# A linear-attention and maxout-FFN kernel: gate weights fetched in two parts each, a halved last tile, and a new order of the steps

## The chip, the core and the metric

The kernel runs on one core of a Trainium2 chip. The metric is the device time of one execution in microseconds (us), lowest first. A core has five instruction streams: TensorE (PE, matmuls), VectorE (DVE), ScalarE (ACT), GpSimd (POOL) and SyncE (SP, which here only issues DMAs). POOL also issues DMAs, those that change the type on the way. All DMAs of the core share 16 DMA engines.

## The reference

Two stages. The first is a recurrent attention with decay over 4 batches, 8 heads, 768 steps and 48 dimensions per head; the second a maxout feed-forward layer on the 3072 tokens of 384 features that the first gives.

```python
for t in range(S):                                  # S = 768
    state = alpha[:, :, t, :, None] * state + k[:, :, t] (outer) v[:, :, t]
    y[:, :, t] = q[:, :, t] @ state
x = y with heads side by side                       # 3072 x 384
h = max(max(x @ w1, x @ w2), x @ w3)                # w: 384 x 768
out = h @ w_out                                     # w_out: 768 x 384
```

Everything comes in and goes out as float32.

## The kernel before

**Tiles.** The sequence is cut into chunks; one *group* `n` (12 of them, three chunk pairs for each of the 4 batches, the batches taking turns) is 256 tokens and two *units* `u = 2n, 2n+1` of four heads each. The products run in fp16.

**Maxout as differences.** The kernel keeps w1 and turns w2 and w3 in place into `w2 - w1` and `w3 - w1` (tile `wcat`). Then `h' = max(0, x(w2-w1), x(w3-w1))`, and the lost part `x w1` goes past the maximum: `out = h' w_out + x (w1 w_out)`. The product `past = w1 w_out` is made once; for it w1 has to be turned (`w1T`) on PE.

**Steps.** `Plan.step` records each piece of work with its operands; nothing is issued then. The steps that the text speaks of, by kind:

- `load` (SP): q, k, v or alpha of a group, 384 KB in rows of 384 bytes (group 0 in halves of 192 KB). `weights` (POOL): a weight, cast from fp32 to fp16 on the way.
- per group: `aa` (alpha pair product), `la` (its logarithm, ACT), `hp` and `e` (chunk totals, PE and ACT), `G` (decay factors).
- per unit: `Lp` (PE, sums of logarithms), `L0` (DVE), two `exp` (ACT), two `qk` (products, DVE or POOL), `v` (scaling, ACT or POOL), `tp` (PE, 16 transposes), `qkT` (DVE), `A` (PE, scores), `LA` (DVE, mask).
- per group: `pp` (PE, new state), `Zp`, `Z`, `add` (DVE or POOL, carry the state), `yi` and `ya` (PE, outputs from the state and within the chunk), `xb` (ACT or DVE), `xp` (PE), `xT` (ACT or DVE): the layer's input, turned.
- once: `d` (DVE, the six differences, of 256 columns each), `wt` (PE, turn w1), `w1T` (copy), `mp` (PE, w1 w_out), `past` (copy).
- per group of the layer: six gate steps `gp(n, j, g)` (PE, six matmuls of 128x128 on 256 columns; `j` is the block of 256 hidden columns, `g` the difference), `h0` and `h1` (the maxima), two `op` (PE, three matmuls with `past` and six with w_out), `ob` (copy of the output tile of 128 tokens) and `out` (SP).

**Order.** The order of all steps is written out in the table `ORDER`. A token such as `254P1` means step 254, on PE, in PSUM bank 1; the letters P, V, A, G and S stand for PE, DVE, ACT, POOL and SP. `Plan.emit` issues the steps in this order, so each engine runs its own steps in the order of the table, and waits where an operand isn't there. Step numbers count the calls of `Plan.step`; `WAFTER` only says at which point of the recording a weight's step is numbered; its place in time is the table's alone.

What a line number in the profile stands for: L262 load, L272 weights, L281 `d`, L294 `wt`, L307 `mp`, L324 `aa`, L329 and L334 `la`, L389 `Lp`, L393 `L0`, L398 `exp`, L403 `qk`, L421 `tp`, L429 `qkT`, L441 `A`, L449 `LA`, L472 `pp`, L509 `yi`, L531 `ya`, L551 `xp`, L575 `gp`, L584/L586 `h0`, L591 `h1`, L603 and L606 the two halves of `op`, L618 `out`; L243 and L247/L249 are helpers for copies and scalings.

Of the kernel before, what the change touches and what calls it, by code (L numbers as in the profile page):

```python
# [10 lines left out]
FP32 = mybir.dt.float32  # L11
# [15 lines left out]
6S 0S 3S 1S 2S 52S 5S 7S 8V 9A 4S 10A 11G 17P0 54S 18V 13A 53S 19A 14P1 98S 28P2 12A 20A 55S 29V  # L27
15A 22V 100S 30A 31A 21V 99S 56V 101S 24P3 16G 143S 58A 32V 145S 57A 33V 74P5 144S 59P6 25V 62P7
35P0 146S 23A 63V 205S 26P2 64A 36V 272S 65A 34A 206S 75V 37P0 67G 27V 207S 60A 40P47 77A 274S 76A
61G 339S 66V 208S 42V 78G 69P2 38V 273S 39G 79V 41V 73G 81P5 68A 102G 82V 70V 83P0 80G 104A 44P4  # L30
85G 84V 86P56 45P2 87V 71P0 88V 46A 119P3 72V 103A 47P5 90P2 49A 120V 91P4 122A 193P0 92V 95A 105P1
121A 89V 108P4 93P2 48A 43V 96P3 50P6 123V 51A 94A 124V 109V 126P5 111A 97A 195P7 189V 106A 187V
196A 262P2 127V 321P3 194A 188V 128P5 110A 113V 254P1 112G 129V 258P7 255A 130G 329P0 115P4 192V
330A 197P1 107G 116V 114A 125G 331P6 198A 190V 117P4 325P0 322A 118V 147G 148A 256P1 191V 149A
131P34 263A 257V 153P5 259A 264P2 154V 133V 326A 132V 164P1 260P7 156A 265V 327P0 165V 261V 167A
135P3 323P2 166A 332V 155A 136P7 324V 169G 201P1 140V 158G 150P6 199P5 202A 137A 157V 151A 168V
160P2 328V 171P6 203P1 159A 170G 172V 200A 161V 173P6 204A 175P05 209G 174V 162P2 333P1 211A 163V
276G 277A 210A 218P6 269P7 334A 152G 219V 539S 278A 176V 275S 134V 221A 340S 177V 220A 141P2 229P3
138P1 341S 285P4 222G 230V 179P0 139A 266P6 142V 406S 231A 286V 342S 232A 223V 288A 234G 279P1
180P2 270A 267V 287A 212P3 178V 392P7 181A 233V 213A 296P6 225P4 280A 215G 184A 297V 236P2 290G  # L40
394P1 226V 299A 298A 237V 301G 182P0 393A 388P4 183V 344A 185P5 343G 238P2 395V 224A 227P6 336P0
186A 228V 289G 235A 389A 214G 239V 217G 390P1 337A 216G 345A 292P5 338S 300G 240P74 473S 293V 363P0
352P2 396P3 408S 353V 241V 474S 354A 463P5 391V 397A 268S 242G 398P6 335S 291A 282G 243V 409S 461P7
464A 281G 364V 302G 407S 399V 366A 459P3 284G 271S 365A 244V 476S 245P1 355A 246P5 460V 307P60 671S
357G 247P 462V 605S 294P2 251A 465P4 283G 295V 248A 356G 252P7 411A 455P5 253A 308V 368G 457P1 456A
466V 249P2 359P6 410G 458V 250A 303P3 346P5 529P2 304V 310G 412A 525P1 360V 309G 347A 530A 367G
305P3 311V 369A 361P5 521P7 306V 526A 349G 350G 358A 312P2 523P0 351G 522A 362V 543G 313P1 413P3
419P4 430P7 314P 414A 431V 370P5 420V 433A 467P3 524V 315A 435G 371V 318A 421A 477G 372P0 422A
374P25 545A 470P6 436G 479A 375V 478A 348G 373V 376G 432A 379P4 434G 480P2 471A 403P7 468A 424V
377V 486P0 319P1 423G 404A 531P6 487V 378V 488A 405S 380P3 527P7 481A 532V 608S 320A 541S 489A 381P  # L50
609G 528V 544A 475S 426P1 437P5 382A 540S 415G 316P0 427V 503G 400P7 317A 438V 416G 385V 383P4
552P1 401V 386P2 384A 591P0 483V 387A 402S 553V 484G 428P5 672S 592A 439P3 675G 497P7 555A 655P2
440V 554A 425G 593P0 611A 485G 498V 589P1 500A 418V 429V 491G 546P3 499A 653P4 587P7 417G 654A 594V
441P56 547A 676A 490V 563P4 533P3 442V 588V 443G 444G 656V 661P0 534A 501G 564V 447P5 535S 663P7
590V 662A 606S 492G 677A 446P2 445V 657P3 674S 565A 502G 664V 542S 566A 493P0 448P 658V 472S 482G
556G 504P6 607S 494V 508P4 624A 469S 659P3 452A 449V 610A 618P0 505V 595P1 450P5 453P2 596V 597P6
451A 454A 509V 536P7 660V 511G 549G 619V 568G 598V 621A 506P1 495P4 620A 678P3 551G 537A 725P6 496V
569G 679A 538S 684P0 612P7 719P3 557G 673S 685V 507V 665P4 567G 550V 686A 629P5 695P1 548V 599P2
510V 613A 720A 681V 623V 666A 615V 683V 723P7 622G 696V 630V 698A 602P3 724V 631A 614G 558G 687A
726V 635A 688G 721P4 697A 600V 603A 512P7 700G 601S 513P0 722V 632A 625P1 667S 514P 604S 626V 699G  # L60
574P6 515A 559P3 570P1 518A 727P5 634G 571V 701A 519P7 575V 729P0 616G 728A 560V 577G 516P1 668P2
633G 517V 730V 520V 627P5 669A 572P3 689V 561P0 737P7 670S 617V 573V 731P2 738A 562V 741P7 732A
578P3 576V 745P4 742A 628V 690A 579P0 636P1 580P 637V 640P7 581A 691P5 584V 638P1 746A 582P3 692V
747P0 583A 641V 644P4 743P5 639V 642G 739P6 643G 680V 585P3 645P7 740V 702P1 586A 646P 682V 706P3
703V 647A 734P6 650A 748V 707V 744V 704P1 709G 693P3 759P7 708G 735V 694V 755P0 757P5 705V 711P6
752P3 710P4 761P1 753A 756A 754S 648P2 712P 760A 733S 651P3 649A 749P0 762V 652A 716V 713V 777P7
750A 763P2 751S 736S 717P1 714P3 781P6 718A 779P4 782V 765P0 715V 783P1 778V 799P6 764V 801P3 766V
800A 773P7 784V 775P2 758V 793P0 780V 797P6 774V 795P1 791P5 767P4 792V 802V 770P7 776V 768A 796V
769S 794V 785P5 798V 771V 803P3 786V 772S 787S 807P4 804P 808P 805V 788P2 809A 806S 810S 789A 790S
# [44 lines left out]
def kernel(  # L114
# [12 lines left out]
    nc = tc.nc  # L127
# [112 lines left out]
    WAFTER = {2: (0,), 4: (1,), 7: (2,), 11: (3,)}  # L240
# [27 lines left out]
    def weights(g):  # L268
        w, dst = ((moe_w1, moe_w2, moe_w3, moe_w_out)[g],
                  (w1s, wcat[:, :, 0, :], wcat[:, :, 1, :], wo16)[g])  # L270
        plan.step("weights", "POOL", -1.0,
                  lambda eng: nc.gpsimd.dma_start(dst, w.rearrange("(t p) f -> p t f", p=P)),  # L272
                  writes=[("w", g)], size=1.25 if g == 3 else 1.0)


    def differences():
        for g in range(2):
            for j in range(NJ // 2):
                cols = slice(2 * j * P, (2 * j + 2) * P)
                plan.step("d", "DVE", LEAD - 0.5 + 0.5 * g,  # L280
                          lambda eng, g=g, cols=cols: nc.vector.tensor_sub(  # L281
                              wcat[:, :, g, cols], wcat[:, :, g, cols], w1s[:, :, cols]),
                          reads=[("w", 0), ("w", g + 1)], writes=[("d", g, j)])


    def bypass():
        rank = LEAD + 0.5 * SLOPE
        for kt in range(NFT):
            wk = ("wt", kt)

            def turn(eng, kt=kt, wk=wk):
                live[wk] = bank(wk, [P, NJ, P], FP16)
                for j in range(NJ):
                    nc.tensor.transpose(live[wk][:, j, :], w1s[:, kt, j * P:(j + 1) * P], ident)  # L294
# [331 lines left out]
    for n in range(NG):  # L626
# [3 lines left out]
        for u in (2 * n, 2 * n + 1):  # L630
            prep(u)
            for j in (2 * u, 2 * u + 1):
                for g in WAFTER.get(j, ()):
                    weights(g)
# [40 lines left out]
```

## Time and profile before

| | us |
|---|---|
| median of three runs | 153.78 (153.15 to 154.35) |
| the profiled execution's own time | 153.0 |
| span of the profiled execution | 151.2 |
| PE busy | 133.5 (88%) |
| DVE busy | 120.7 (80%) |
| ACT busy | 82.3 (54%) |
| POOL busy | 69.3 (46%) |
| PE's chain share: gate matmuls (L575) | 31% |

The span is what the profiler saw from the first to the last instruction; the execution's own time holds some 1.8 us more around it. A page of the profile has the span in 40 slices (3.78 us each, a digit for the busy tenths), the chain of work that ended last, groups of instructions by line, and the DMA queues: q1 is SP's (loads and outputs), q0 is POOL's (weights). A row of the timeline or chain gives the start, the length, and what ran; in brackets how long the engine stood before it and what ended that.

### The profile page before, as it was taken

Reading aid. Unit: us, or ns where it says so; the run is one execution under the profiler, and the core shown is the slowest. Engines: PE = TensorE matmul, PEld = TensorE weight load, DVE = VectorE, ACT = ScalarE, POOL = GpSimd, SP = SyncE. Lnnn points to the kernel's source line nnn. Section 1 sums busy time; section 2 is a strip of 40 time slices with the busy share of each in tenths; the row PEclk is TensorE's granted clock in tenths of the full one; section 3 lists DMA queues with packets and bytes.
Section 4 is the critical chain, followed back from the end, with each engine's and each line's share of the span. In section 5 each row is a group of like instructions: output and inputs, shape, how many; then the busy total and the mean of one; then the engine's idle time right before and its main releaser. Section 6 shows DMA issues by size and latency. Waiting matters only on the chain.

```text
span 151.2 us, 5265 instructions
## 1 busy us (share of the span) xinstructions
PE 133.5 (88%) x2220; PEld 102.4 (68%) x2220; DVE 120.7 (80%) x210; ACT 82.3 (54%) x185; POOL 69.3 (46%) x106
## 2 busy tenths in 40 slices
PE   0145498999999999999999999998999999999991
PEld 0133276677766778888677878766868877888660
DVE  3188988769999999999698998899899992395920
ACT  3467246829576996777967756536627305210111
POOL 8114920080390697798992865688800220000000
PEclk9999999999999999999999999999999999999999
DMA  5999999999999999999529929960410002300124
GB/s 127 273 261 261 266 213 211 240 249 221 279 260 262 262 252 261 282 310 270 114 59 259 290 60 259 255 191 0 160 56 0 4 4 81 127 4 0 52 104 156
DMA packets 55880, 26.45 MB, mean 175 GB/s; under 512 B 50737, under 2 KB 55857, under 8 KB 55857
## 3 DMA queue, kind: packets, MB, share of 16 engines
q1 hardware_dynamic: 53440, 23.60, 63.5%
q0 software_dynamic: 1984, 2.36, 9.0%
q8 instruction: 17, 0.28, 0.8%
q10 hardware_dynamic: 432, 0.17, 0.5%
q14 instruction: 7, 0.05, 0.1%
HBM read 23.76 MB, written 4.72 MB: 188 GB/s over the span
## 4 chain that ended last, share of the span: by engine, by line
PE 74%; DMA 11%; SPq 5%; DVE 3%; issue 3%; ACT 2%; POOL 1%; ACTq 0%; DVEq 0%; POOLq 0%
PE psum L575 31%; PE psum L606 14%; PE psum L603 7%; DMA wcat<-in_moe_w_dram 7%; SPq L262 5%; PE psum L441 4%; DMA qn<-in_q_dram 4%; PE psum L421 4%; PE psum L531 3%; PE psum L472 3%; PE psum L551 2%; PE psum L307 2%; PE psum L509 2%; PE psum L389 1%; DVE Z L373 1%
## 5 line engine op out<-in xcount | busy, mean ns | idle before, releaser
L575 PE MATMUL psum<-xT,wcat 128*128 128x256 f16 x432 | 55.3, 277 | 0.3 <-DVE wcat L281 0.3
L575 PEld LDWEIGHTS <-wcat 128*128 128x128 f16 x432 | 40.7, 99 | 6.6 <-DVE wcat L281 0.5
L449 DVE TENSOR_TENSOR LA<-psum,d 128x1024 f16<-128x1024 f32 x24 | 28.8, 1219 | 3.8 <-PE psum L441 2.6
L606 PE MATMUL psum<-wo,hT 128*128 128x384 f16 x144 | 27.3, 326 | 0.0
L591 DVE TENSOR_TENSOR hT<-psum,hT 128x512 f16<-128x512 f32 x36 | 23.8, 681 | 3.2 <-PE psum L531 2.8
L403 POOL TENSOR_TENSOR qk<-qn,ep 128x384 f16<-128x384 f32 x16 | 16.7, 1052 | 14.5 <-ACT ep L398 14.0
L243 ACT COPY ob<-psum 128x384 f32<-128x384 f32 x17 | 8.1, 484 | 24.7 <-PE psum L606 24.7
L403 POOL TENSOR_TENSOR qk<-kn,en 128x384 f16<-128x384 f32 x15 | 15.0, 1001 | 13.0 <-ACT en L398 8.5
L606 PEld LDWEIGHTS <-hT 128*128 128x128 f16 x144 | 14.1, 98 | 9.3
L584 ACT ACTIVATE hT<-psum 128x512 f16<-128x512 f32 x25 | 14.6, 600 | 8.1 <-PE psum L575 7.9
L429 DVE COPY qkT<-psum 128x1024 f16<-128x1024 f16 x24 | 16.0, 684 | 1.4 <-PE psum L421 1.1
L603 PE MATMUL psum<-past,xT 128*128 128x384 f16 x72 | 15.7, 327 | 0.0
L421 PE MATMUL psum<-d,qk 64*128 64x64 f16 x384 | 10.6, 200 | 5.2 <-DVE qk L403 4.0
L398 ACT ACTIVATE en<-psum 128x384 f32<-128x384 f32 x24 | 11.8, 496 | 5.3 <-DVE psum L393 4.1
L398 ACT ACTIVATE ep<-psum 128x384 f32<-128x384 f32 x24 | 11.7, 492 | 4.6 <-POOL qk L403 2.9
L373 POOL TENSOR_TENSOR Z<-U,G 48x192 f16<-48x192 f32 x12 | 6.0, 504 | 16.3 <-DVE U L486 15.8
L421 PEld LDWEIGHTS <-qk 64*128 64x128 f16 x384 | 8.1, 100 | 8.0 <-DVE qk L403 5.3
L243 ACT CAST xT<-psum 128x384 f16<-128x384 f32 x19 | 8.8, 483 | 6.0 <-PE psum L551 5.7
L324 POOL TENSOR_TENSOR aa<-an 128x384 f32<-128x384 f32 (+1 forms) x11 | 10.7, 972 | 2.6 <-DMA an<-in_alpha_dram 2.5
L247 ACT ACTIVATE xb<-psum,c 128x384 f16<-128x384 f32 x17 | 9.4, 580 | 4.2 <-PE psum L531 4.1
L586 DVE TENSOR_SCALAR hT<-psum 128x512 f16<-128x512 f32 x11 | 7.5, 686 | 4.4 <-PE psum L575 4.3
L247 ACT ACTIVATE v<-vn,c 128x384 f16<-128x384 f32 x14 | 8.6, 617 | 4.3 <-DMA vn<-in_v_dram 3.9
(54 smaller groups left out, 193.8 us busy)
## 6 DMA issues: line engine op xcount, KB each, us to landing
out_dram<-ob SPq DMA_DIRECT2D x24, 192.0 KB, 2.0
an<-in_alpha_dram SPq DMA_DIRECT2D x11, 384.0 KB, 6.1
kn<-in_k_dram SPq DMA_DIRECT2D x11, 384.0 KB, 5.9
qn<-in_q_dram SPq DMA_DIRECT2D x11, 384.0 KB, 6.5
vn<-in_v_dram SPq DMA_DIRECT2D x11, 384.0 KB, 6.1
wcat<-in_moe_w_dram POOLq DMA_DIRECT2D x2, 576.0 KB, 11.3
w1s<-in_moe_w_dram POOLq DMA_DIRECT2D x1, 576.0 KB, 8.0
wo<-in_moe_w_out_dram POOLq DMA_DIRECT2D x1, 576.0 KB, 7.6
```

Source lines behind the costliest of these rows:

```text
L243: (nc.scalar.copy if eng == "ACT" else nc.vector.tensor_copy)(out=out, in_=in_)
L247: nc.scalar.activation(out=out, in_=in_, func=AFT.Copy, scale=factor)
L398: lambda eng, t=t, sign=sign: nc.scalar.activation(out=t, in_=live[Lk], func=AFT.Exp, scale=sign),
L403: lambda eng, w=w, x=x, e=e: on[eng].tensor_mul(qk[:, w, :, :, :D].rearrange("p r h d -> p h r d"), ld[x][n % NL][:, hs], e),
L421: nc.tensor.transpose(live[tk][:, i, at:at + HALF], qk[rows, w, r, 2 * j:2 * j + 2, :], ident[rows, rows])
L429: lambda eng: nc.vector.tensor_copy(out=qkT.rearrange("p i w j t -> p i (w j t)"), in_=live[tk]),
L449: lambda eng: nc.vector.tensor_mul(LA.rearrange("p a j r t -> p (a j) (r t)"), live[Ak].rearrange("p a (j t) -> p (a j) t", j=2), maskA.un ...
L575: nc.tensor.matmul(live[gk][:, jj, :], wcat[:, kt, g, c0:c0 + P], xT[:, kt, :], start=(kt == 0), stop=(kt == NFT - 1))
L584: nc.scalar.activation(out=h, in_=live[gk], func=AFT.Relu)
L591: lambda eng, h=h, gk=gk: nc.vector.tensor_max(h, live[gk], h),
L603: nc.tensor.matmul(live[ok], xT[:, kt, i * P:(i + 1) * P], past[:, kt, :], start=(kt == 0), stop=False)
L606: nc.tensor.matmul(live[ok], hT[:, kt, i * P:(i + 1) * P], wo16[:, kt, :], start=False, stop=(kt == NJ - 1))
```

## The change

1. Each gate weight (w1, w2, w3) comes in two transfers: columns 0 to 255, and columns 256 to 767. `weights(g, part)` takes a part; w_out stays whole. POOL so issues seven weight transfers instead of four.
2. A difference `d` of block `j = 0` reads only the first parts. The turning of w1 (`wt`) goes by blocks of 256 columns instead of blocks of 128 rows, so that its first step reads the first part alone; each copy `w1T` then fills two of the six column blocks. Each `mp` step now reads all three `w1T` copies instead of one.
3. The last output tile (of 24) is made in two halves of 192 columns, each with its own PSUM bank, copy and output transfer; for the second half the output buffer is the next one.
4. A new table `ORDER`, which also gives steps to other engines.

```diff
-    WAFTER = {2: (0,), 4: (1,), 7: (2,), 11: (3,)}
+    WAFTER = {2: (0, 1), 4: (2, 3), 7: (4, 5), 11: (6,)}
...
-    def weights(g):
+    def weights(g, part):
...
+        cols = slice(0, DM) if g == 3 else (slice(0, 2 * P), slice(2 * P, DF))[part]
         plan.step("weights", "POOL", -1.0,
-                  lambda eng: nc.gpsimd.dma_start(dst, w.rearrange("(t p) f -> p t f", p=P)),
-                  writes=[("w", g)], size=1.25 if g == 3 else 1.0)
+                  lambda eng: nc.gpsimd.dma_start(
+                      dst[:, :, cols], w.rearrange("(t p) f -> p t f", p=P)[:, :, cols]),
+                  writes=[("w", g, 1)[:2 + part]], size=1.25 if g == 3 else (1 + part) / 3)
...
     def differences():
-        for g in range(2):
-            for j in range(NJ // 2):
+        for j in range(NJ // 2):
+            for g in range(2):
...
-                          reads=[("w", 0), ("w", g + 1)], writes=[("d", g, j)])
+                          reads=[("w", x, 1)[:2 + (j > 0)] for x in (0, g + 1)], writes=[("d", g, j)])
...
     def bypass():
-        for kt in range(NFT):
-            wk = ("wt", kt)
-            def turn(eng, kt=kt, wk=wk):
-                live[wk] = bank(wk, [P, NJ, P], FP16)
-                for j in range(NJ):
-                    nc.tensor.transpose(live[wk][:, j, :], w1s[:, kt, j * P:(j + 1) * P], ident)
+        for j in range(NJ // 2):
+            wk = ("wt", j)
+            def turn(eng, j=j, wk=wk):
+                live[wk] = bank(wk, [P, 2, DM], FP16)
+                for a in range(2):
+                    for kt in range(NFT):
+                        c0 = (2 * j + a) * P
+                        nc.tensor.transpose(live[wk][:, a, kt * P:(kt + 1) * P],
+                                            w1s[:, kt, c0:c0 + P], ident)
...
-                      lambda eng, kt=kt, wk=wk: copy(eng, w1T[:, :, kt * P:(kt + 1) * P],
-                                                     live[wk]),
+                      lambda eng, j=j, wk=wk: copy(eng, w1T[:, 2 * j:2 * j + 2, :], live[wk]),
...
-            plan.step("mp", "PE", rank, product, banks=[mk], reads=[("w1T", kt), ("w", 3)],
-                      writes=[mk])
+            plan.step("mp", "PE", rank, product, banks=[mk],
+                      reads=[("w1T", j) for j in range(NJ // 2)] + [("w", 3)], writes=[mk])
...
+            wide = 1 if m < NG * UB - 1 else 2
+            for half in range(wide):
+                cols = slice(half * DM // wide, (half + 1) * DM // wide)
+                ok = ("op", m, 1)[:2 + half]
+                home = (m + half) % 4
...
+                            live[ok] = bank(ok, [P, cols.stop - cols.start], FP32)
...
+                              eng, obs[home][:, cols], live[ok]),
...
+                              out[rows, cols], obs[home][:, cols]),
...
-                for g in WAFTER.get(j, ()):
-                    weights(g)
+                for at in WAFTER.get(j, ()):
+                    weights(*((0, 0), (1, 0), (2, 0), (0, 1), (1, 1), (2, 1), (3, 0))[at])
```

Five stretches of the two order tables, in words (numbers are groups for `aa`, `G`, `hp`, and units for the rest):

| | before | after |
|---|---|---|
| POOL, up to the third weight's first transfer | `aa` 0, `G` 0, `qk` of unit 2, `G` 1, `qk` of unit 3, **w1**, **w2**, `aa` 2, `v` of unit 3, **w3**; then a `qk` of unit 4, **w_out** | `aa` 0, `aa` 2, `G` 0, `qk` of unit 2, `v` of units 1 and 2, `G` 1, **w1 first part**, **w1 second**, **w2 first**, `qk` of unit 4, **w2 second**, **w3 first**; then two `qk` of unit 5, `aa` 3, **w3 second**, **w_out** |
| PE, from `ya` of group 1 to the first gate step | `ya`, `wt`, `hp` 2, `Lp` 4, three `xp`, `tp` 5, `wt`, gate step of group 0, block 2 | `ya`, `tp` 4, `xp`, `A` 4, `wt`, `xp`, `wt`, `tp` 5, `wt`, gate step of group 0, block 0 |
| PE, next | gate step of group 1, `A` 5, two gate steps | gate step of group 1, `A` 5, two gate steps of blocks 2 and 1 (second parts) |
| SP, loads after group 0's | a1, k1, q1, a2, v1, k2, q2, v2, a3, k3, q3, v3, a4 ... | a1, a2, q1, k1, v1, k2, q2, a3, v2, k3, q3, a4, a0', v3 ... |
| PE, at the end | `op` of tile 22 and of tile 23 without their last two matmuls, those two each, `op` of tile 21 whole | `op` of tile 22, first half of tile 23, their last two each, `op` of tile 21 whole, second half of tile 23 |

In the SP row, a1 is alpha of group 1, and so on; a0' is the alpha that takes group 0's buffer again (group 5). In the first row of the table of tokens, for example, `3S 0S 5S 6S 53S 2S 11G 12A 1S 13A 8V` opens the new order and `6S 0S 3S 1S 2S 52S 5S 7S 8V 9A 4S` the old one.

## The prediction

> **What bounds the kernel now.** I read the slices of the span first, then the stretches, then PE's waits, the chain, and last the DMA queues.
>
> ```profile
> PE   0145498999999999999999999998999999999991
> DMA  5999999999999999999529929960410002300124
> ```
>
> TensorE (PE) is full from the eighth slice to the last but one. So two things can be shortened: the time until PE is full, and what follows its last matmul. The stretches and PE's waits after 28 us say how full:
>
> ```profile
> 20.00:25.00 5.00, 4.59 (x115) 3.97 (x112) 3.84 (x7) 2.91 (x7) 0.00 (x0) 1.00 1.15 209
> 25.00:28.14 3.14, 2.52 (x31) 1.77 (x30) 2.37 (x7) 2.46 (x8) 0.00 (x0) 1.00 1.15 210
> 28.14:32.00 3.86, 3.86 (x34) 2.62 (x35) 2.46 (x5) 1.65 (x3) 2.10 (x4) 1.00 1.11 261
> ```
> ```profile
> PE psum L421 <- ACT ep L398: 0.5, 1, 0.5
> PE psum L575 <- DVE wcat L281: 0.3, 1, 0.3
> ```
>
> After the columns for time, PE comes first. From 28.14 us PE waits 0.8 us in 120. What set that start is in the chain of work that ended last (start, length, what):
>
> ```profile
> 14.49 1.37 POOL qk L403
> 15.93 0.84 issue
> 16.76 10.67 DMA wcat<-in_moe_w_dram
> 27.53 0.57 DVE wcat L281
> 28.14 2.74 PE psum L575 x12
> ...
> 31.43 2.07 PE psum L575 x18
> ```
>
> The first gate matmuls (L575) waited for w2: issued by GpSimd (POOL) at 16.76, landed at 27.43, one subtraction, start at 28.14. Beside that, the first 12 gate matmuls take 228 ns each and the next 18 take 115: until about 31.4 us PE runs at half pace, though the clock column says 1.00 throughout.
>
> The queues from 22 to 28 us (packets, MB, share):
>
> ```profile
> q0 software_dynamic: 665, 0.99, 90.4%
> q1 hardware_dynamic: 661, 0.25, 24.1%
> ```
>
> While weights (q0) and loads (q1) both wait, they take turns packet by packet, whatever their size. From 19 to 21 us, at the start, the weights had 254 packets to the loads' 124. So a load that isn't through when the weights begin is held: v of group 2, issued at 15.65, landed 15.6 us later.
>
> **The change part by part.** The profiled execution took 153.0 us, 151.2 of it span; the median of the runs is 153.78, so I make the sum against 153.0 and add 0.78.
>
> *1. Start of the weights: 2.5 us later.* In the new POOL order two copies of v stand ahead of the first weight, the second on the v load of group 1. Loads come in at 0.753 us per 192 KB (k of group 1, the 12th such unit, at 12.99; v of group 1, the 18th, at 17.3). The second v is the 18th again: 17.5, plus 0.59 for the copy (L249 row) and 0.2 for G, so the first weight is issued at 18.3 instead of 15.81. Before, the first weight packets show 2.8 us after the issue; so 21.1 now. By then k and q of group 2 and alpha of group 3 are in, and most of v of group 2, now the 26th unit. Behind it in SP's queue stand k and q of group 3 and alpha of group 4, which take turns with the weights; counted by the turns below they land near 30.5, 36 and 40, and POOL and DVE have work for them from about 36, 39 and 43.
>
> *2. The weights in seven pieces.* Each of the three gate weights keeps its 384 packets in either part, of a third and of two thirds of the size. Cost of a packet: 1,536 bytes written at 127 a us on 16 engines is 126 ns; w_out's of 768 bytes ran at 237 a us, 67 ns; the line through both gives 47 ns at 512 and 86 at 1,024. In turn with the loads, 144 ns were seen (111 a us) for the large one, so 18 more: 65 and 104 ns. With 25 packets per engine: 1.6 us for a first part, 2.6 for a second, 4.2 for a whole weight against 3.6 before. The first piece runs alone (1.2 us, to 22.3), the second nearly half alone (to 24.7), w2's first part to 26.4. Landing follows the last packet by 1.8 us (w1: packets through at about 22.0, landed at 23.8). So w1's parts land at 24.1 and 26.5, w2's at 28.2 and 30.8, w3's at 32.4 and 35.0, w_out at 39.2 (before: 23.8, 27.4, 31.0, 38.5). First gate data are ready at 28.2 + 0.55 for a subtraction: 28.8, later than before. Bounds: with bytes in place of packets sharing evenly, 27.5 for w2's first part; with 67 and 126 ns a packet, 30.1.
>
> The three more issues cost POOL 3 x 0.85 = 2.6 us between 18 and 28. Behind them wait qk of units 4 and 5, done at 25.5 by the rows (1.0 each); PE asks for unit 5 at 28.1, so they lie hidden with 2.6 us to spare.
>
> *3. PE's way to the first gate step.* Walking the new order with the rows of before, group 1's ya starts at 23.25 (before 23.09): k of group 1 lands at 15.2 (15 units), then DVE has three products (1.65), two subtractions (0.7), two qkT (1.4), four Zp (1.4) and one LA (1.2), to 21.6; the second LA waits for its scores until 21.95 and takes 1.22. Then come at the slow pace: ya 0.82, tp4 0.61, xp 0.35, A4 0.64, wt0 0.82, xp 0.35, wt1 0.82, tp5 0.61, wt2 0.82, sum 5.84, and 0.45 waiting for xb and qkT: the first gate step starts at 29.5. The weights' 28.8 is covered by this work; without the cover it would be the start. That is 1.36 us later than 28.14, but tp4, A4 and wt2 are done already, worth 0.34 + 0.35 + 0.44 = 1.13 at the fast pace. Net **+0.23**. w2's second part (30.8) comes before the third gate step, w3's parts before PE's place for them (about 36 and 38), w_out (39.2) before mp (41): nothing there.
>
> *4. The rest of the order table.* I added up the rows along each engine's new order, from the first gate step on. No PE step comes before the engine that makes its operand has got to it; ten stand within 1 us, down to 0.24, where the old order has seventeen, down to 0.03, and hardly waits. DVE has 7 us less work (ten copies and scalings went to ACT), POOL 4.6 more at 46% busy. Tightest chain: tp of unit 14, whose decay sum Lp stands 3.4 us ahead, against 3.0 for subtraction, exponential and two products on POOL. I take 0; bounds -0.8 (all of today's waits) and +2 (two such chains 1 us late).
>
> *5. The tail.* Today:
>
> ```profile
> 147.91 0.48 ACT L243 COPY ob<-psum 128x384 f32<-128x384 f32 x1 [1.03 <-PE psum L606]
> ```
>
> Then an issue of 0.36 and 1.8 to 1.9 us to landing. The last copy has 192 columns: less 0.16, by the two L334 forms (0.36 and 0.52). The transfer is halved: 0 to 0.3 less; I take 0.06. 18 matmuls of 192 columns replace 9 of 384 (163 ns each): the neighbours step at 57 (128 columns) and 109 ns (256), so 83, and 1.49 for 1.47; bounds 1.03 and 1.96. Together **-0.2**, from -0.9 to +0.4.
>
> Sum: 153.0 + 0.23 - 0.2 = 153.0, and on the scale of the median **153.8**: no change. A measurement of this kernel tells about 1% (1.5 us) from none.
>
> **The rivals.**
>
> *PE gets fast early (faster).* The new order gives PE nearly unbroken work from 22.7 us; the old one stood for 0.4 us before ya and 0.6 before the gate step. If unbroken work is what ends the slow pace, it ends before the first gate step: that then starts at 28.8 (the weights), 0.7 earlier, and its first 12 matmuls take 1.3 instead of 2.74. Gain 2.1 us: 151.7. For it: the pace doubled after 3.2 us of unbroken matmuls. Against it: from 24.5 to 27.9 us PE was busy for 3.02 of 3.4 and stayed slow.
> [...]
>
> *The weights come late (slower).* Twice as many packets take turns with the loads. With 67 and 126 ns a packet, w2's first part lands at 30.1 and the first gate step starts at 30.8 (+1.3); w2's second part lands 3.6 us on and holds the third step for 0.3; w3's second part 0.5, w_out 0.5. Together 2.6 on top of the sum: 156.4. It decides from a landing of w2's first part after 28.9. The start of the weights belongs to it: each us that v of group 1 is late counts. For it: the turns by packet, and the later issue. Against: the packets of w_out were half as long as those of w1.
> [...]
>
> *The middle tears (a little slower).* One or two chains as in 4 come late: +1 us, 154.8. For it: one new order for some 800 steps; against it: the sums.
>
> That the halves of a weight wait for each other is excluded: in the built program the first subtraction waits for the first and the third weight transfer alone.
>
> **How the numbers follow.** No change 0.42; PE fast early 0.23; weights late 0.25; middle torn 0.10, half of it over 1%. The forecast itself spills 0.02 on either side. Faster 0.25, within 1% 0.43, slower 0.32. The forecast's own range is 152.5 to 155.2; to hold 8 in 10 the range goes to the fast rival (151.7, with its tail 151.3) and the slow one (156.4).
>
> **What would show it.** First weight issued near 18.3; w2's first part landed near 28.2; first gate step near 29.5 with matmuls of 220 ns, fast from about 32.7; PE's waits after that under 1 us; last copy near 0.32 us. It is wrong if the gate steps start fast, if PE stands before the first or third gate step for the weights, or if PE waits over 1 us after 33 us.

## The result, and the profile after

The changed kernel takes 157.93 us (median of 4 runs, 157.69 to 158.34) against 153.59 of before beside it: ratio 1.028, 95% interval 1.0232 to 1.0328. That is 4.3 us slower, where the prediction had no change. The profiled execution took 157.82 us with a span of 156.0, 4.8 more than before's 151.2. Before's median moves from session to session (153.1 to 153.6 us), so every ratio below is to before's runs of the same session, and leaves out runs over 1.5% above the fastest of their kernel.

Lines move by 1 to 10 in the changed kernel: weights L274, `d` L284, `wt` L299, `aa` L329, `Z` L378, `qk` L408, `tp` L426, `qkT` L434, `A` L446, `LA` L454, `yi` L514, `ya` L536, `gp` L580, `h1` L596, `op` L613/L616. The slices (3.9 us each) and the stretches:

```profile
PE   0236798999989995499999999999999999999992
DMA  5999999999999999998199992325200000030054
```
```profile
20.00:25.00 5.00, 4.57 (x117) 3.44 (x115) 4.17 (x7) 3.34 (x7) 4.96 (x7) 1.00 1.28 223
25.00:29.38 4.38, 3.80 (x53) 2.81 (x54) 2.21 (x4) 1.52 (x4) 3.52 (x5) 1.00 1.24 204
29.38:32.00 2.62, 2.62 (x24) 1.75 (x28) 1.58 (x4) 1.99 (x4) 0.00 (x0) 1.00 1.27 206
59.80:64.40 4.60, 0.97 (x9) 0.64 (x8) 4.54 (x3) 1.55 (x4) 4.25 (x5) 1.00 1.04 262
64.40:68.70 4.30, 4.28 (x86) 3.53 (x87) 3.48 (x7) 1.05 (x2) 0.50 (x1) 0.64 1.17 314
```

The start looks as forecast. The hole is in the middle: from 59.8 to 64.4 us PE works for 0.97 of 4.60 us, while DVE and POOL both look busy (4.54 and 4.25). Behind it PE is full, at a mean clock of 0.64 (1.00 until about 65.5, then 0.50 until about 69). PE's waits from the first gate step on, and the chain (start, length, what):

```profile
PE psum L514 <- DVE Z L378: 3.6, 1, 3.6
PE psum L426 <- DVE qk L408: 0.4, 1, 0.4
PE psum L580 <- DVE wcat L284: 0.2, 1, 0.2
```
```profile
20.08 8.60 DMA wcat<-in_moe_w_dram
28.77 0.57 DVE wcat L284
29.38 2.50 PE psum L580 x12
...
59.83 4.45 DVE Z L378
```

One wait stands out, and one DVE instruction makes it: token `246V`, the second half of the carried state `Z` of unit 8's group (48x192). DVE's timeline, and POOL's beside it:

```profile
59.12 0.68 DVE L596 TENSOR_TENSOR hT<-psum,hT 128x512 f16<-128x512 f32 x1
59.83 4.44 DVE L378 TENSOR_TENSOR Z<-U,G 48x192 f16<-48x192 f32 x1
```
```profile
59.74 0.50 POOL L378 TENSOR_TENSOR Z<-U,G 48x192 f16<-48x192 f32 x1
60.21 0.99 POOL L408 TENSOR_TENSOR qk<-qn,ep 128x384 f16<-128x384 f32 x1
61.17 0.99 POOL L329 TENSOR_TENSOR aa<-an 128x384 f32<-128x384 f32 x1
62.12 0.99 POOL L408 TENSOR_TENSOR qk<-qn,ep 128x384 f16<-128x384 f32 x1
63.07 0.99 POOL L408 TENSOR_TENSOR qk<-kn,en 128x384 f16<-128x384 f32 x1
```

A `Z` of DVE takes 0.35 us in the median. Here it started 0.09 us after POOL's half of the same state and ended 0.2 us after POOL's run of five instructions. A wait for an operand shows as idle time ahead of the row that waited (3.64 us in PE's row below), and this row has none. PE then pays twice. It stands for 3.64 us, and a little later its matmuls are slow: behind the stand 8 of `yi` and six of a gate step still take what they take elsewhere (0.50 and 0.82 us), but the next six of a gate step take 1.46.

```profile
64.42 0.50 PE L514 MATMUL psum<-Z,qkT 128*128 128x96 f16 x8 [3.64 <-DVE Z L378]
64.75 0.82 PE L580 MATMUL psum<-xT,wcat 128*128 128x256 f16 x6
...
67.27 1.46 PE L580 MATMUL psum<-xT,wcat 128*128 128x256 f16 x6
```

The tail, where before showed 0.48:

```profile
153.16 0.32 ACT L244 COPY ob<-psum 128x192 f32<-128x192 f32 x1 [1.85 <-PE psum L616]
```

### The profile page after: what moved, and what is told of

Read it like the earlier page. It is cut to its first block, busy times and chain, and to the rows that moved or that the text cites. A ratio compares the mean times of both kernels' runs of the same rounds, so it can differ in the third digit from the quotient of the medians.

```text
span 156.0 us, 5288 instructions
## 1 busy us (share of the span) xinstructions
PE 136.5 (87%) x2229; PEld 104.1 (67%) x2229; DVE 118.0 (76%) x199; ACT 86.1 (55%) x194; POOL 72.3 (46%) x112
## 4 chain that ended last, share of the span: by engine, by line
PE 72%; DMA 9%; DVE 7%; SPq 7%; POOL 1%; issue 1%; ACT 1%; DVEq 0%
PE psum L580 30%; PE psum L616 15%; PE psum L613 8%; SPq L263 7%; DMA wcat<-in_moe_w_dram 6%; PE psum L446 4%; DMA vn<-in_v_dram 4%; PE psum L426 3%; DVE Z L378 3%; PE psum L477 3%; PE psum L556 3%; PE psum L536 3%; PE psum L514 2%; DVE hT L596 1%; DVE qk L408 1%
## 5 line engine op out<-in xcount | busy, mean ns | idle before, releaser
L580 PE MATMUL psum<-xT,wcat 128*128 128x256 f16 x432 | 55.7, 278 | 0.4 <-DVE wcat L284 0.2
L580 PEld LDWEIGHTS <-wcat 128*128 128x128 f16 x432 | 40.8, 99 | 7.2 <-DVE wcat L284 0.5
L596 DVE TENSOR_TENSOR hT<-psum,hT 128x512 f16<-128x512 f32 x36 | 24.1, 684 | 8.0 <-PE psum L580 6.9
L454 DVE TENSOR_TENSOR LA<-psum,d 128x1024 f16<-128x1024 f32 x24 | 28.7, 1216 | 1.4 <-PE psum L446 1.1
L616 PE MATMUL psum<-wo,hT 128*128 128x384 f16 (+1 forms) x150 | 27.5, 320 | 0.0
L408 POOL TENSOR_TENSOR qk<-kn,en 128x384 f16<-128x384 f32 x16 | 16.1, 1008 | 15.9 <-ACT en L403 15.5
L589 ACT ACTIVATE hT<-psum 128x512 f16<-128x512 f32 x29 | 17.0, 601 | 11.7 <-PE psum L580 11.7
L616 PEld LDWEIGHTS <-hT 128*128 128x128 f16 x150 | 14.5, 98 | 8.9
L434 DVE COPY qkT<-psum 128x1024 f16<-128x1024 f16 x24 | 16.2, 686 | 3.8 <-PE psum L426 3.8
L408 POOL TENSOR_TENSOR qk<-qn,ep 128x384 f16<-128x384 f32 x16 | 15.9, 996 | 6.7 <-ACT ep L403 4.8
L244 ACT COPY ob<-psum 128x384 f32<-128x384 f32 (+1 forms) x19 | 8.8, 474 | 16.3 <-PE psum L616 16.3
L248 ACT ACTIVATE xb<-psum,c 128x384 f16<-128x384 f32 x21 | 11.5, 582 | 11.3 <-PE psum L536 11.1
L613 PE MATMUL psum<-past,xT 128*128 128x384 f16 (+1 forms) x75 | 15.8, 320 | 0.0
L426 PE MATMUL psum<-d,qk 64*128 64x64 f16 x384 | 11.2, 204 | 4.5 <-DVE qk L408 3.6
L426 PEld LDWEIGHTS <-qk 64*128 64x128 f16 x384 | 8.3, 102 | 7.9 <-DVE qk L408 5.3
L329 POOL TENSOR_TENSOR aa<-an 128x384 f32<-128x384 f32 (+1 forms) x10 | 10.1, 1007 | 7.6 <-DMA an<-in_alpha_dram 7.4
L244 ACT CAST xT<-psum 128x384 f16<-128x384 f32 x20 | 9.5, 479 | 7.4 <-PE psum L556 7.2
L378 POOL TENSOR_TENSOR Z<-U,G 48x192 f16<-48x192 f32 x12 | 6.3, 523 | 14.5 <-DVE U L491 14.2
L394 PE MATMUL psum<-la,c 128*128 128x192 f16 x24 | 6.0, 267 | 6.8 <-ACT la L339 6.8
L446 PE MATMUL psum<-qkT 48*64 48x128 f16 x384 | 9.9, 239 | 0.8 <-DVE qkT L434 0.7
```

The source lines that it names most:

```text
L244: (nc.scalar.copy if eng == "ACT" else nc.vector.tensor_copy)(out=out, in_=in_)
L408: lambda eng, w=w, x=x, e=e: on[eng].tensor_mul(qk[:, w, :, :, :D].rearrange("p r h d -> p h r d"), ld[x][n % NL][:, hs], e),
L426: nc.tensor.transpose(live[tk][:, i, at:at + HALF], qk[rows, w, r, 2 * j:2 * j + 2, :], ident[rows, rows])
L434: lambda eng: nc.vector.tensor_copy(out=qkT.rearrange("p i w j t -> p i (w j t)"), in_=live[tk]),
L446: nc.tensor.matmul(live[Ak][i * HALF:(i + 1) * HALF, p, at:at + P], qkT[rows, i, 1, j, r * HALF:(r + 1) * HALF], qkT[rows, i, 0, j, :], st ...
L454: lambda eng: nc.vector.tensor_mul(LA.rearrange("p a j r t -> p (a j) (r t)"), live[Ak].rearrange("p a (j t) -> p (a j) t", j=2), maskA.un ...
```

## The experiments

The theory to begin with: a DVE instruction with two operands in SBUF cannot start while POOL works without a gap. The rivals: the split weights or the later start cost it; the step waited for data; many small waits add up. Three kernels and a set of bare trials came first.

**e1: the held step on POOL.** In after's table

```
-245G 459A 462P1 542S 246V 358A
+245G 459A 462P1 542S 246G 358A
```

> One step of the order table of after is moved: the second half of the carried state of unit 8 (Z <- U,G, 48x192), which DVE held for 4.44 us at 59.83 us, is given to POOL, right behind the first half. Everything else is after's. Theory (a DVE instruction with two operands in SBUF cannot start while POOL works without a gap): POOL does it in 0.50 us, PE's wait of 3.64 us before L514 falls under 1 us, and the slow matmuls behind that wait (about 1.5 us more) go too; the time falls from 157.9 to 153.0 (152.3 to 154.3), level with before or below it. Rival 1 (the split weights and the later start cost it): stays at 157 or more, since nothing of the start is touched. Rival 2 (the step waited for U or G, so for data): POOL waits as long as DVE did, and the time stays at 157 or more. Rival 3 (many small waits of the new order add up): falls by the 3.6 us of the one wait at most, if PE then waits elsewhere by less still: 155 or more.

Measured: 152.83 us (10 runs), ratio to before 1.0011 (0.9978 to 1.0044); span 151.2, as before's. PE's waits from the first gate step on:

```profile
PE psum L580 <- DVE wcat L284: 1.1, 1, 1.1
PE psum L426 <- DVE qk L408: 0.3, 1, 0.3
```

One letter of the table is the whole loss. The scores (L446) that start at 55.06 us in after start at 55.25 here; those behind the hole start at 71.25 and at 66.40. So the hole costs 5.04 us: 3.64 of wait, and 1.40 left over for the slow matmuls. The rest of the change is worth +0.2 us, from -0.3 to +0.7. All three rivals fall. (The 1.1 us before the first gate step is new: in this execution PE ran fast from 22.7 us on, `ya` in 0.58 us where after took 0.82, and so was there sooner; more of that at the end.)

**e2: two of POOL's five instructions taken out.**

```
-... 338S 413G 368A 463V 250P ... 398V 411S 359G
+... 338S 368A 463V 413V 250P ... 398V 359V 411S
```

> After, with the held step still on DVE, but two of the five POOL instructions that ran without a gap beside it (one aa and one qk, 0.99 us each) given to DVE behind it (0.55 us each there). POOL's stretch is then Z, qk, qk: 0.50 + 2 x 0.96 us from 59.74, ending near 62.2. Theory (held until POOL stops): the step takes 2.5 us instead of 4.44, PE's wait before L514 falls from 3.64 to about 1.7 us, and the time falls by 2 to 3.5 us, to 154.5 to 156. If it is held for one POOL instruction only and the rest of the 4.44 us has another cause (data, a slow instruction): 4.4 us as before, time 157 to 158. If the step gets in between two POOL instructions: under 1.6 us, and the time near 153.5.

Measured: 155.25 us, ratio 1.0117 (1.0052 to 1.0182). DVE's row, POOL's rows and PE's:

```profile
60.30 2.54 DVE L378 TENSOR_TENSOR Z<-U,G 48x192 f16<-48x192 f32 x1
```
```profile
60.21 0.51 POOL L378 TENSOR_TENSOR Z<-U,G 48x192 f16<-48x192 f32 x1
60.68 0.99 POOL L408 TENSOR_TENSOR qk<-qn,ep 128x384 f16<-128x384 f32 x1
61.63 0.99 POOL L408 TENSOR_TENSOR qk<-kn,en 128x384 f16<-128x384 f32 x1
```
```profile
62.99 0.50 PE L514 MATMUL psum<-Z,qkT 128*128 128x96 f16 x8 [1.75 <-DVE Z L378]
...
65.16 0.83 PE L580 MATMUL psum<-xT,wcat 128*128 128x256 f16 x6
```

Two instructions fewer, 1.90 us less: the step ends when POOL's run does, with the same data from the same producers. And after 1.75 us of standing PE keeps its full pace (0.83, clock 1.00); after 3.64 it did not.

**e3: the same put into before.** `283G 295V` becomes `283V 295V`.

> Before, with one step moved the other way: a half of the carried state of unit 9 (Z <- V,H, 48x192), which POOL did at 63.52 us, is given to DVE at the same place of the table, where it arrives near 63.6 beside three POOL instructions (qk, qk, aa) that then run without a gap to about 66.5. Theory: DVE's Z takes up to 2.9 us instead of 0.35, DVE's next step (LA) starts near 66.5 instead of 63.57, PE waits for it or for the step behind it by 1 to 2.5 us more than now, and the time rises by 1 to 3.5 us, to 154.8 to 157. If what after lost had to do with its data or with its other parts and not with the neighbour on POOL: Z takes 0.35 us (or under 1.1, as the longest of before), and the time stays at 153.3 to 154.2.

Measured: 154.25 us, ratio 1.0042 (1.0004 to 1.0081). The step took 1.16 us, not 2.9: it got in after one POOL instruction, though POOL's qk, qk, aa (64.05, 65.00, 66.08) had no pause. DVE's row, and POOL's first two, of which the second is 0.11 us longer than usual:

```profile
64.09 1.16 DVE L373 TENSOR_TENSOR Z<-V,H 48x192 f16<-48x192 f32 x1
```
```profile
64.05 1.00 POOL L403 TENSOR_TENSOR qk<-qn,ep 128x384 f16<-128x384 f32 x1
65.00 1.11 POOL L403 TENSOR_TENSOR qk<-kn,en 128x384 f16<-128x384 f32 x1
```

So "held while POOL works without a gap" was wrong as it stood.

**e4: bare trials.**

> No part of the reference is computed: 26 small trials, one after the other. In each, a ScalarE copy releases at once a chain of POOL instructions without a gap and a DVE filler of 24 to 384 columns on PSUM, behind which one DVE instruction of the disputed kind stands: Z (48x192, two operands in SBUF), P (the same with one operand in PSUM) or Q (128x384, two operands in SBUF). Chains: none, 1, 2, 3, 5 and 8 of qk's multiplication (0.96 us each), the sequence of after (Z, qk, aa, qk, qk) with three fillers, four qk with four fillers, four aa, four Z, four of the one-operand v, eight of the small G, and mixtures. Theory (a lock that POOL keeps while its instructions follow without a gap): Z without a chain 0.35 us; with 1, 2, 3, 5, 8 qk it ends when the chain does (up to 7.5 us for 8); P is never held (0.35 us); Q is held as Z is. Rival (held for the one POOL instruction that was running, then let in): Z takes at most 1.3 us whatever the length of the chain. Rival (nothing to do with POOL): 0.35 us in all trials. The small G and the one-operand v tell whether POOL's instruction needs two operands, or a full width, to hold DVE.

Measured, DVE's instruction, length in us (alone: Z 0.35, qk 0.55; fillers of 24 to 192 columns):

| POOL's run beside it | Z of DVE | other |
|---|---|---|
| 1, 2, 3, 5, 8 x qk | 0.91, 0.86, 0.85, 0.86, 0.85 | qk beside 4 x qk: 1.06 |
| 4 x aa / Z / v, 8 x G | 0.86 / 0.47 / 0.46, 0.35 | |
| Z, qk, aa, qk, qk | 3.22, 3.32, 3.40, 3.32 | qk: 3.64 |
| either, one operand in PSUM | | 0.36, 0.36 |

In these trials DVE was held with both operands in SBUF (0.85 us and more beside qk, 3.22 and more beside Z, qk, aa, qk, qk) and not with one in PSUM (0.36 beside either). Beside eight qk it was let in after the first (0.85 us); beside Z, qk, aa, qk, qk it stayed out (3.22 to 3.64). DVE's row and POOL's, of the first trial of that run (line numbers of the trials are their own):

```profile
30.66 3.22 DVE L646 TENSOR_TENSOR Z<-U,G 48x192 f16<-48x192 f32 x1
```
```profile
30.31 0.50 POOL L646 TENSOR_TENSOR Z<-ep,G 48x192 f16<-48x192 f32 x1 [0.62 <-ACT ep L684]
30.77 0.98 POOL L643 TENSOR_TENSOR qk<-qn,ep 128x384 f16<-128x384 f32 x1
31.72 0.99 POOL L651 TENSOR_TENSOR aa<-qn,ep 128x384 f32<-128x384 f32 x1
32.67 2.06 POOL L643 TENSOR_TENSOR qk<-qn,ep 128x384 f16<-128x384 f32 x2
```

It got in between the two equal qk, which write the same place: they stand 1.07 us apart (four of them take 4.21 us beside the DVE step with one operand in PSUM), those with places of their own 0.95.

**e5: in after, POOL's qk ahead of its Z.** `... 460P4 274S 245G 459A ... 358A 292G 461V` becomes `... 460P4 292G 274S 245G 459A ... 358A 461V`; DVE keeps `246V`.

> After with one exchange in POOL's queue: the qk step that followed the first half of the carried state of unit 8 (Z <- U,G) now runs ahead of it, so that POOL is in a qk (59.74 to 60.7 us) and not in a Z when DVE's half of the same Z arrives at 59.83 us. DVE keeps its half, and POOL's work is as gapless as in after. The earlier run in which a Z of DVE arrived beside qk, qk, aa was held for one POOL instruction only (1.16 us). Theory A (DVE gets in at the end of the running POOL instruction, except where that is a Z): DVE's Z takes 1.2 to 1.3 us, PE waits about 0.9 us before L514, the time is 153.3 to 154.5. Theory B (any gapless stretch of POOL holds DVE to its end): Z takes 4 us or more, the time stays at 157 to 158.5.

Measured: 153.32 us, ratio 1.0038 (1.0003 to 1.0073); DVE's Z took 0.75 us at 60.09. POOL's rows:

```profile
59.63 1.00 POOL L408 TENSOR_TENSOR qk<-qn,ep 128x384 f16<-128x384 f32 x1
60.59 0.62 POOL L378 TENSOR_TENSOR Z<-U,G 48x192 f16<-48x192 f32 x1
61.18 0.99 POOL L329 TENSOR_TENSOR aa<-an 128x384 f32<-128x384 f32 x1
```

DVE was let in at 60.59; POOL's Z took 0.12 longer for it, and PE waited 0.2 us. POOL is as gapless as before, with the same instructions. It is their order that counts.

**e9, e10: what about Z does it?** Two more sets of trials, each POOL instruction writing a place of its own.

> No part of the reference is computed: 24 trials as in the first set of trials, but every instruction of a POOL chain now writes a tile (or half of one) of its own. There a Z of DVE was let in after one qk, aa, Z or v when the next POOL instruction was of the same kind, and held for three instructions more in the chain Z, qk, aa, qk, qk, to the boundary of the two equal ones. Here the first instruction is varied (Z on 48 partitions, qk, aa, v, the small G, a Z on 128 partitions y, a half-long product h, a product on 48 partitions n), with qk, aa, qk, aa behind it, and the place of the Z in the chain. Theory A (a Z that is running when DVE asks makes it miss every boundary up to the end of the chain): chains that begin with Z hold DVE's Z for 3 us and more, those that begin with qk, aa, v or G for at most 1.3 us; y, h and n tell whether it is the 48 partitions, the broadcast operand or the short duration. Theory B (it is the next instruction: DVE is let in where the next one writes the same tile and so waits for the one before): every chain holds DVE to its end, 2.5 to 4.5 us, whatever it begins with; a chain one instruction longer holds 0.96 us longer. Theory C (DVE is let in after the running one, always): at most 1.3 us everywhere. P, one operand in PSUM, 0.36 us in all theories.

> No part of the reference is computed: 29 trials as in the second set. There every chain of POOL that began with Z (48 partitions, one operand repeated along its row) held DVE to the chain's end, 0.96 us longer for each instruction more, while chains that began with qk, aa, v, G, a Z on 128 partitions, a half-long product or a product on 48 partitions with no repeated operand let DVE in after one instruction. Here the first instruction is Z on partitions 64 to 111 (1), on 64, 96 and 32 partitions (2, 3, 4), on 48 without the repeated operand (5), twice as long on 128 and on 48 partitions (6, 7), a half-long product on 128 (8) and a long one on 48 (9). If it is the 48 partitions: 1, 5, 7 and 9 hold DVE for 4 us as z does, 6 and 8 do not. If it is the repeated operand with fewer than 128 partitions: 1, 2, 3, 4 and 7 hold, 5, 6, 8 and 9 do not. If it is partitions 0 to 47 being short of the DVE instruction's own 64 to 111: 1 does not hold. D is a DMA issue of 192 columns: a run above held a qk of DVE for two POOL instructions where a DMA issue and qk, qk, aa followed each other, with no Z near; if the DMA issue is a second trigger, the three trials with D hold for 2 us and more, otherwise at most 1.3 us. Late arrivals (fillers of 384 and more): DVE asks beside the second or third POOL instruction, so that a Z that is over by then still counts or does not.

Measured (Z of DVE unless said, behind the named first instruction qk, aa, qk, aa or three of them):

| POOL's run | DVE's instruction, us |
|---|---|
| Z / Z, qk / Z, qk, aa / Z, qk, aa, qk / Z and six more | 0.46 / 1.41 / 2.37 / 3.39 / 6.17 |
| first qk / v / G | 0.95 / 0.56 / 1.11 |
| first qk or aa, Z as second, DVE asking in the first | 0.95, 0.96 |
| DVE asking in the qk behind a Z that is over | 3.97, 3.02 |
| first on 32, 64, 96 partitions; on 48 without the repeated operand | 4.26, 4.27, 4.27; 4.35 |
| first on 128 partitions, 0.51, 0.59, 0.83 long | 0.47, 0.55, 0.79 |
| first on 48 partitions, 0.82 long / 0.99 long | 4.59 / 1.01 |
| first on partitions 64 to 111 | 0.47 |
| qk, DMA issue, then qk, qk, aa, aa (DVE: a qk) | 3.88, 4.40, 3.50 |
| DMA issue, POOL standing 0.24 us, then qk, aa, qk, aa | 0.66 |
| full-width only, DVE asking in the second instruction | 0.61, 0.61 |
| Z, then v (one operand) | 0.62 |

Theories B and C of e9 fall, and so does "it is the Z": other instructions on 32 to 96 partitions do it (4.26 to 4.59 us), and a DMA issue does (3.50 to 4.40). Theory A falls as worded, since the instruction can be over when DVE asks (3.97 and 3.02 us). Two rows fitted no single idea: 48 partitions at 0.99 us let DVE in, and so did partitions 64 to 111, where POOL itself stood for 0.07 us behind the instruction.

**e12: out of step.** The first of the two rows gave the last theory.

> No part of the reference is computed: 15 trials as before, on why a short POOL instruction on few partitions shuts DVE out. Theory (a run out of step): the lanes of POOL that have nothing to do in an instruction on partitions 0 to 47 go on to the next one at once, so that from there to POOL's next pause some lanes are always in the middle of an instruction, and there is no boundary at which DVE could be let in. Then it hangs on the length of the short instruction against the period of those behind it (0.955 us start to start): a product f on 48 partitions and 96, 144, 192, 240, 288, 336 and 360 columns (0.25 to 0.93 us), followed by qk, aa, qk, aa, qk, holds DVE's Z to the end of the run, 4.5 us and more, but with 384 columns (0.955 us, in step again) for 1.0 us only. A Z on 48 partitions followed by four Z of 128 partitions, each into a tile of its own (0.46 us apart, as long as the first), is in step again: 0.5 us. A Z followed by four more on 48 partitions: nothing runs on the other lanes, so every end is a boundary: 0.5 us, and with qk, aa behind these five the same. Rival (any instruction on few partitions shuts DVE out until POOL pauses): every one of these chains holds Z to its end, 2 to 5 us. Z, qk, aa, qk, aa, qk again 5.2 us and the chain of 128-partition Z alone 0.5 us in both.

Measured: with 96, 144, 192, 240, 288, 336 and 360 columns 5.10, 5.20, 5.30, 5.40, 5.50, 5.60 and 5.65 us; with 384 columns 1.01 and 1.08. Z and four Z on 128 partitions: 0.52 and 0.60. Z and four Z on 48 partitions: 0.47, with qk and aa behind them 0.47. All as the theory has it, and against the rival in six of the trials (sixteen, the one with 192 columns having run with a second filler, 5.37 us). The two neighbours, 360 columns and 384 (POOL's rows):

```profile
44.33 0.94 POOL L671 TENSOR_TENSOR xb<-ep,qn 48x360 f16<-48x360 f32 x1 [1.14 <-ACT ep L699]
45.23 0.98 POOL L645 TENSOR_TENSOR qk<-qn,ep 128x384 f16<-128x384 f32 x1
...
51.15 0.98 POOL L671 TENSOR_TENSOR xb<-ep,qn 48x384 f16<-48x384 f32 x1 [1.14 <-ACT ep L699]
52.10 1.16 POOL L645 TENSOR_TENSOR qk<-qn,ep 128x384 f16<-128x384 f32 x1
```
```profile
44.58 5.65 DVE L648 TENSOR_TENSOR Z<-U,G 48x192 f16<-48x192 f32 x1
...
51.40 1.01 DVE L648 TENSOR_TENSOR Z<-U,G 48x192 f16<-48x192 f32 x1
```

24 columns, 0.05 us from start to start, decide over 4.6 us. At 384 columns the first instruction is as long as the period of those behind it; DVE comes in at its end, and the qk shows that by its 1.16 us.

**e6: the split undone** in e1's kernel; the second parts' steps issue nothing.

```
-lambda eng: nc.gpsimd.dma_start(dst[:, :, cols], w.rearrange(...)[:, :, cols])
+lambda eng: part or nc.gpsimd.dma_start(dst, w.rearrange("(t p) f -> p t f", p=P))
```

> The version of after with the held Z on POOL (152.83 us), with one part of the change undone: each of w1, w2, w3 comes in one transfer again, issued where its first part was (w1 at 18.4 us, w2 at about 20, w3 at about 22); differences, turned copy, tail and the order table stay. Before's two whole weights landed 11.7 us after the first was issued, so the first difference waits to about 30 and the first gate step starts at 30.3 to 31.5 us instead of 29.55. If the split is worth what the prediction gave it (1.13 us of gate work earlier): time 153.3 to 154.8. If the start doesn't matter, because PE would have had to wait anyway: 152.6 to 153.1.

Measured: 153.37 us, ratio 1.0024 (0.9987 to 1.006), not to be told from e1. DVE's row (L282 is `d` in this kernel):

```profile
29.03 0.56 DVE L282 TENSOR_TENSOR wcat<-wcat,w1s 128x768 f16<-128x768 f16 x1 [0.82 <-DMA wcat<-in_moe_w_dram]
```

The whole w2, issued at 18.93, is there at 28.97; in after its first third, issued at 20.08, at 28.68. So the split brings the first difference 0.3 us at most. The first gate step starts at 29.73 (e1 29.55, after 29.38), and here it isn't the weights that set it: PE comes straight from the turning of w1, with no wait. The time falls at the edge of the first forecast, but with no difference from e1 that could be told, so the split's worth in time stays open. (After and e1, with one and the same table up to there, are 0.17 us apart themselves.)

**e7, e11: the tail alone.** e7 is e1's kernel with the last tile whole; e11 is before with the two halves, its table ending `809A 806S 811P6 810S 789V 812P 790S 813A 814S`.

> The version of after with the held Z on POOL (152.83 us), with the last output tile in one piece again: its six-plus-three matmuls of 384 columns, one copy, one transfer, at the place of the first half in the table. The prediction gave the halves 0.2 us: 153.0 to 153.2, which the comparison may not tell from no change; in the trace the last copy takes 0.55 us instead of 0.32, and the stretch from the last matmul to the end of the span is 0.2 to 0.4 us longer. If the halves cost (18 more weight loads, 6 more matmuls): 152.3 to 152.7.

> Before, with one part of the change alone: the last output tile in two halves of 192 columns, at the end of before's own order table (the second half behind the tile that was last). The prediction gave this 0.2 us; in the traces of the version with the Z on POOL, with and without halves, the stretch from the last transposed-state step to the end of the span is 33.7 and 34.2 us, so 0.4. Expected: 152.7 to 153.1 against 153.1 to 153.3 of before, at the edge of what the comparison tells; last copy 0.32 or 0.36 us instead of 0.48. If the 18 more weight loads and the smaller matmuls cost what the shorter copy saves: no difference, or 0.2 us more.

Measured: e7 153.51 us, ratio 1.0054 (1.0022 to 1.0086); e11 152.66 us, ratio **0.9951 (0.9914 to 0.9988)**. The stretch from the last scores (L446, before L441) to the end of the span is 33.72 us in e1 and 34.15 in e7, 28.83 in e11 and 29.23 in before: the halves save 0.4 us in either table. In whole times e7 can't be told from e1. e11 is faster than before by an interval that just stays below 1, and its profiled execution (span 149.8) owes another 1.0 us to a start that went faster (the last scores at 120.97 us against 121.97), which has nothing to do with the halves.

**e8: earlier weights.** In e1's kernel `39G 75G 40G` moved behind `67G`, `74G` ahead of `116G`.

> A try for a version that beats both: after with the held Z on POOL, and in POOL's queue w1's two parts and w2's first part put behind the qk step that ends at 14.7 us, ahead of two v steps for which POOL waits 1.5 and 0.9 us, and w3's first part ahead of one qk step. They are issued at 14.7 to 17.3 us instead of 18.34 to 20.9, land 2 to 3.5 us earlier, and the first gate step can start at 26 to 28 us instead of 29.55. What speaks against it: 768 KB more stand ahead of the loads of q, k and v on the same DMA engines, so that these land up to 3 us later while PE still waits for them. If the weights are what PE lacks from 24 to 30 us: 150.5 to 152. If the loads are: 152.5 to 154.

Measured: 157.41 us, ratio 1.0298 (1.0254 to 1.0341), slower than either forecast. The first gate step starts at 34.50 us, not at 26 to 28. One of PE's waits (L564 is `xp` in this kernel):

```profile
PE psum L564 <- ACT xb L256: 5.1, 1, 5.1
```

Alpha of group 3, issued at 15.85, landed 13.3 us later; ACT stood for it in `la` for 6.6 us, with xb queued behind. So in this order a load, not a weight, holds the start.

## Why the prediction was wrong

**The step that failed is step 4**, "The rest of the order table ... I take 0; bounds -0.8 and +2". It added up rows along each engine, one length for each kind of instruction, and looked for operands that come late. `246V` was in it with some 0.35 us. What it took was 4.44 us, for a cause that no operand shows: what its neighbour runs. The +2 was a bound on late chains, and was too near by 3 us for the same reason. By e1 that one step costs 5.04 us, all of the span's 4.8 and a little more. The sums of work themselves held: in e1 DVE has 6.9 us less than in before (7 in the forecast) and POOL 3.5 more (4.6).

The trace of before had the sign: the same step took 0.64 us beside POOL there, a `qk` of DVE at 75.48 us 1.10 instead of 0.55, and another `Z` three times its median:

```profile
76.61 1.04 DVE L373 TENSOR_TENSOR Z<-U,G 48x192 f16<-48x192 f32 x1
```

I read the medians.

**Rival "The middle tears"** was right in kind, at +1 us and 0.10. It was priced as a chain that is late, not as an engine that is shut out.

**Step 1** (18.3): 18.34, the v load having landed at 17.57 for 17.5 (the two rows that it quotes lie 0.72 us a unit apart and not 0.753, a difference of 0.2 us over the six). **Step 2**: w2's first part at 28.68 for 28.2, its second near 31.4 for 30.8, w1's second at 27.0 for 26.5; some half a microsecond late throughout, for which PE waited 0.33 us (w1's second part) and 0.25 us (the first difference). **Step 3** (first gate step 29.5): 29.38, with matmuls of 208 ns for 220, fast from 31.8 for 32.7. With e1's +0.2 us (-0.3 to +0.7) for everything but the held step, the net of steps 1 to 3 and 5, 0.0 in the forecast, is inside what was measured. How far the gain in step 3 and its later start cancel was not measured one by one.

**Step 5** (-0.2): -0.4 by the traces, -0.75 (-1.3 to -0.2) by the comparison of e11. Mis-sized, in the right direction. (Its upper bound adds up to +0.3, not +0.4: -0.16 and 0.49.)

**"PE gets fast early"**: not in after's trace. The first 12 gate matmuls took 2.50 us (2.74 before) though PE had been busy for 8.4 of the 9.4 us ahead of them. But it is a matter of the execution, not of the table alone: e11 has before's start and e1 has after's, and both ran fast early (`ya` of group 1 in 0.57 us at 23.25 and in 0.58 at 22.71, where before and after took 0.82). e11 kept that pace. e1 lost it: its clock was 0.50 from about 29.4 to 32.6 us. Their first 12 gate matmuls, e11's and then e1's:

```profile
28.34 1.48 PE L575 MATMUL psum<-xT,wcat 128*128 128x256 f16 x12 [1.16 <-DVE wcat L281]
29.55 2.74 PE L580 MATMUL psum<-xT,wcat 128*128 128x256 f16 x12 [1.08 <-DVE wcat L284]
```

So the rival's fast gate steps do occur, near its price (1.3 us for the 12), and one trace of each kernel could not settle it. What slowed e1 was not shown: from 25.9 us until its gate step at 29.55 PE ran only `tp` and `wt`, all transposes, and it also stood twice in that time (1.29 and 1.08 us); no run separates the two. **"The weights come late"**: no, 28.68 is before 28.9.

**The slow matmuls behind the hole** were in nobody's sum. They followed a stand of 3.64 us (clock 0.64 in the stretch behind it) and not one of 1.75 (e2: 1.00). At e1's start shorter stands among transposes (1.29 and 1.08 us) came before a slow clock too (0.50). What makes the clock fall was not shown.

## What to carry to other kernels

A table of instruction lengths was not enough here to place work on DVE and POOL: an instruction of DVE with both operands in SBUF beside a run of POOL's qk and aa cost what was left of the running POOL instruction on top of its own length (a `Z` of 0.35 us alone took up to 1.16 us), and the whole rest of the run where a shorter instruction on the first 32 to 96 partitions, or a DMA issue, had come ahead in it (4.44 us in after, up to 6.17 in the trials). So look in a new order for such steps next to POOL runs that contain a short instruction on part of the partitions or a DMA issue, and give them to POOL (e1: 152.83 us for 157.93), put a full-width instruction ahead of the short one where the DVE step asks (e5: 0.75 us for 4.44), or read one operand from PSUM (0.36 us in the bare trials, and 0.36 at most for the eight `Z` of after that read PSUM). When one instruction's longest is many times its median (4.44 to 0.35 us here), look at its neighbours' timeline before its operands.

## What the runs showed of the hardware

- POOL's qk and aa (128x384) with places of their own followed each other 0.955 us apart at 0.99 us of length; DVE got in at such a boundary (in all 0.95 us beside qk, aa, qk, aa, qk, and 0.61 where it asked later in the running instruction) although the trace shows no gap.
- After an instruction on partitions 0 to 31, 47, 63 or 95 that was shorter than the next ones (4.26 to 4.59 us in e10), or after a DMA issue (3.50 to 4.40), it didn't, until POOL paused: up to 6.17 us beside seven instructions. In e12 it hung on the length of that instruction against the period of the next ones (5.65 us at 360 columns, 1.01 at 384). That idle lanes run ahead was the author's theory, which foretold all of e12's trials; the lanes themselves are in no trace, and for the DMA issue no run tests it.
- DVE was held with both operands in SBUF; with one in PSUM its `Z` took 0.36 us beside the same runs (e4).
- Left open: why POOL stood for 0.07 us behind an instruction on partitions 64 to 111, where DVE's `Z` took 0.47 us.
